# Block 0's rows and V's first weights loaded in two halves on two queues, and V's first steps split at 128 columns

## The chip, the cores and the metric

The kernel runs on one core of a Trainium2 chip. The metric is the device time of one execution in microseconds; the figure quoted for a kernel is the median of several runs.

## What is computed

A token block of 2048 rows and 512 columns in bf16 is layer-normalised and then goes through two mixers whose results are added to the input: a sliding dilated attention (32 heads of 16, a window of 8 positions 2 apart) and a gated MLP with a mixing over positions.

```python
xn = _layernorm(x)
# A: attention
q, k, v = split(xn @ wqkv)                     # 512 -> 3 x 512
logits = einsum('bhsd,bhswd->bhsw', q, kg) * Dh ** -0.5   # kg, vg: rows s, s-2, ..., s-14
o = einsum('bhsw,bhswd->bhsd', softmax(where(mask, logits, -1e9)), vg)
a = o @ wo
# B: gated MLP
z = gelu(xn @ w_in)                            # 512 -> 2 x 896
z1, z2 = z[..., :896], layernorm(z[..., 896:])
g = einsum('ts,bsf->btf', w_sp, z2) + b_sp     # 2048 x 2048 over positions
b = (z1 * g) @ w_out
out = x + a + b
```

## The kernel before

The 2048 rows are 16 blocks of 128 (`NB`), and four of them make a wave of 512 (`NJ` = 4). The program is a list of tasks. Each names its engine, what it reads and writes, an estimated duration and a priority. A planner (`Plan.schedule`, L123) places the tasks in an order for each engine, from the estimates and from given landing times of some loads (the dictionary at L1089), and `Plan.emit` writes that order out with semaphore waits. Extra order edges at L1073 to L1086 fix the sequence of the first steps by hand.

The work runs in these stages on TensorE: V's projection of the first blocks; the z2 half of the MLP's input (`z2_block`, L831); Q and K (`qk_pair`, L723); the z1 half (`z1_group`, L877); the rest of V (L700); the attention's reductions (L767); the mixing over positions (`g_group`, L977, the largest); and the output (`out_block`, L1033 and L1042). VectorE does the products of attention, ScalarE the evictions and activations, GpSimd some small steps and V's stores. Most loads go out on SyncE's queue (SP); ScalarE's queue carries two loads at the start and one store at the end.

What the change touches is the first five microseconds:

- Loads. ScalarE issues `ldx0` (L562, the 128 rows of block 0, 128 KB) and `ldx1` (L535). SP issues `ldwv0` and `ldwv1` (`ld_wv`, L539: V's weights, two halves of 256 KB; half `hf` holds the 128-row chunks 2 `hf` and 2 `hf` + 1), then `ldx2`, `ldx3`, `ldwin2a` and `ldwin2b` (L545, L551), `ldx4`, and then DMA transposes `xTd1` and on (L640). Each load has a semaphore of its own.
- Warm-up. TensorE runs seven matmuls on constants (L581; six of 512 columns, one of 128) and an eighth of 128 columns between the transposes and V's first step.
- ScalarE runs a priming activation (`actprime`, L585), before which its function table is loaded.
- Blocks 0 to 2 aren't normalised ahead of V: their raw rows are transposed on TensorE (`pe_tr`, L600) into PSUM, copied by ScalarE to the tile `xcT` (L628), and multiplied with V's weights (`v_block`, L700); mean and variance are put right later (`fix_all`, L751). The contraction over 512 columns goes in four chunks of 128, `dc` = 0 to 3.
- For block 0, `xTx0a` transposes chunks 0 and 1 and `xTx0b` chunks 2 and 3; `xTc0_0` and `xTc0_1` copy 256 columns each; `V0_0` multiplies chunks 0 and 1 (after `xTc0_0` and `ldwv0`), `V0_1` chunks 2 and 3 (after `xTc0_1` and `ldwv1`).
- TensorE's fixed order is: seven warm-up matmuls, `xTx0a`, `xTx0b`, the eighth, `V0_0`, `xTx1`, `V0_1`, `xTx2`, `V1_0`, `V1_1`, `xTr0`, `V2_0`, `V2_1`, then the z2 matmuls of the first blocks.
- VectorE takes statistics of each block (L620, L622), and GpSimd a power for the inverse deviation (L634).

Of the kernel before, what the change touches and what calls it, by code (L numbers as in the profile page):

```python
# [346 lines left out]
def build_kernel(nc, A_x, A_wqkv, A_wo, B_x, B_w_in, B_w_sp, B_b_sp, B_w_out, out, report=False, emit=True):  # L347
# [12 lines left out]
    NRAW = 3  # L360
    NWARM = 7
# [49 lines left out]
    with ExitStack() as es:  # L411
# [5 lines left out]
        def A(name, n, o2_=0):  # L417
            return ar[:, off[name] + o2_: off[name] + o2_ + n]
# [18 lines left out]
        def R1(key, name, n, o_=0):  # L437
            R(key, "sb", [(off[name] + o_, off[name] + o_ + n)])
# [117 lines left out]
        def ld_wqk(which, eng):  # L556
# [5 lines left out]
        dma("act", lambda e: e.dma_start(A("xin", 512), x2[0:128, :]), 128 * 512 * 2, ("xin", 0),  # L562
            writes=[("xin0", 0), ("xin0", 1)], name="ldx0")
        ld_x(1, "act")
        ld_wv(0)
        ld_wv(1)
        ld_x(2, "sp")
        ld_x(3, "sp")
# [45 lines left out]
        def ln_block(b):  # L614
            sl = b % 8
            xin = A("xin", 512, 512 * b)
            xn = A("xn", 512, 512 * sl)
            xk = [("xin", b)] if b else [("xin0", 0), ("xin0", 1)]

            T("dve", lambda v: v.bn_stats(Fv("st6", 6, 6 * b), xin), reads=xk, writes=[("st6", b)],  # L620
              est=685, name="bnst%d" % b, prio=b * 0.1)
            T("dve", lambda v: v.bn_aggr(Fv("mv", 2, 2 * b), Fv("st6", 6, 6 * b)), reads=[("st6", b)],  # L622
              writes=[("mv", b)], est=178, name="bnag%d" % b, prio=-1 + b * 0.1)
            if b < NRAW:
                bcs = [pe_tr(xin, xk, "xTx0a", (0, 1)), pe_tr(xin, xk, "xTx0b", (2, 3))] if b == 0 else [pe_tr(xin, xk, "xTx%d" % b)] * 2
                for h0, hn in ((0, 1), (1, 1)) if b < 2 else ((0, 2),):
                    bc = bcs[h0]
                    T("act", (lambda h0, hn, bc: lambda a: a.activation(A("xcT", 256 * hn, 512 * b + 256 * h0),  # L628
                                                                        P(bc, 256 * hn, 256 * h0), ACTF.Copy))(h0, hn, bc),
                      reads=[bc], writes=[("xcT", b, hf) for hf in range(h0, h0 + hn)], est=c_act(256 * hn),  # L630
                      name="xTc%d_%d" % (b, h0), prio=-1)
# [58 lines left out]
        def v_block(b):  # L690
            bk = plan.bank("V%d" % b)
            sl = b % 8
            vk = ("Vn", sl)
            vn = A("Vn" if sl < 4 else "bbc", 512, 512 * (sl % 4))

            for hf in range(2):
                def mm(t, hf=hf):
                    last = None
                    for dc in (2 * hf, 2 * hf + 1):
                        last = t.matmul(P(bk, 512), A("xcT", 128, 512 * b + 128 * dc) if b < NRAW else xTv(b, dc),  # L700
                                        A("wv", 512, 512 * dc), start=(dc == 0), stop=(dc == 3))
# [13 lines left out]
            v_write(b, vn, vk)  # L715
# [355 lines left out]

        byname = {t.name: t for t in plan.tasks}
        for names in (["warm%d" % wi for wi in range(NWARM)] +  # L1073
                      ["xTx0a", "xTx0b", "warm%d" % NWARM, "V0_0", "xTx1", "V0_1", "xTx2", "V1_0", "V1_1", "xTr0", "V2_0", "V2_1",
                       "z2_0_0", "z2_0_0b", "z2_0_1", "z2_1_0", "z2_1_1", "z2_2_0", "z2_2_1", "V3_0", "V3_1", "z2_3_0", "z2_3_1", "V4_0", "V4_1", "z2_4_0", "z2_4_1", "Q0_0", "Q0_1", "K0_0", "K0_1"],
                      ("rstd7", "Vw3"),
                      ("bnst0", "bnag0", "vpe0", "bnst1", "bnag1", "vpe1", "norm0", "bnst2", "norm1", "bnag2", "vpe2", "bnst3", "norm2",
                       "bnag3", "vpe3", "norm3", "bnst4", "bnag4", "vpe4", "mr", "norm4", "bnst5"),
                      ["bnst%d" % b for b in range(5, NB)],
                      ("xTc0_0", "xTc0_1", "xTc1_0", "xTc1_1", "xTc2_0", "xTe0_0", "xTe0_2", "Ve1", "Ve0", "Ve2",  # L1080
                       "z2g0", "z2g1", "z2s0"), ("ldx4", "xTd1", "xTd2", "xTd3", "xTd4", "ldq", "ldk", "ldx5", "ldx6", "ldx7", "ldwin1", "ldx8"), ("ldx15", "xTd5"),
                      *[("ldwin1", "ldx%d" % b) for b in range(9, NB)], *[("z2_4_1", "%s0_%d" % (n, c)) for n in "QK" for c in range(4)],
                      ("V10_1", "Q3_3"), ("csa", "csb", "csc", "csr", "ldwout"), ("csr", "ldwo0"), ("csr", "ldxr0"), ("csv", "zr3")):
# [4 lines left out]
        plan.schedule(tol=4.0, dma_bw=285.0, dma_lat=1600.0, overlap=60.0,  # L1088
                      land=dict(ldx0=3600.0, ldwv0=4120.0, ldx1=4550.0, ldwv1=5230.0, ldx2=5600.0, ldwin2a=7650.0, ldx3=6050.0,  # L1089
                                ldwin2b=8950.0, csa=75800.0, csb=78400.0, csc=83400.0, csr=86500.0, ldx4=9100.0, ldx5=18150.0, ldq=16300.0, xTd3=12130.0, ldk=17800.0, ldx6=18500.0, ldx7=18900.0, xTd4=13900.0, xTd1=9600.0, xTd2=10850.0, ldwin1=21500.0))  # L1090
        if report:
            print("arena", AR, "fp", FR)
# [12 lines left out]
        plan.landed = {("dve", "fin11_0"): [("wv", 0), ("wv", 1), "w_in2a", "w_in2b", "w_in1", "bbc", "w_out", "wo", ("xin", 0), ("xin", 1), ("xin", 2), ("xin", 3), ("xin", 4), ("xin", 5), ("xin", 6), ("xin", 7), ("xin", 8), ("xin", 9), ("xin", 10), ("xin", 11), ("xin", 12), ("xin", 13), ("xin", 14), ("xin", 15), ("wv", 0), ("wv", 1), "w_in2a", "w_in2b", "w_in1", "bbc", "w_out", "wo", ("xin", 0)]}  # L1105
# [36 lines left out]
```

## Time and profile before

| | |
|---|---|
| median of 3 runs | 236.19 us (235.75, 236.23, 236.19) |
| the profiled execution | 236.54 us |
| its span | 235.3 us, 3002 instructions |
| TensorE matmuls | 232.4 us busy, 99% |
| VectorE | 207.3 us, 88% |
| ScalarE | 95.9 us, 41% |
| GpSimd | 29.4 us, 12% |
| transfers | 44.55 MB, mean 189 GB/s |

The span runs from the first to the last instruction of the core; the execution's time has some 1.2 us around it. A line of the profile names the engine (PE is TensorE, PEld its weight loads, DVE VectorE, ACT ScalarE, POOL GpSimd, SP SyncE; a small q marks an engine's sequencer or its DMA issue), the source line, the operation, what is written and read, the shape and the count. In a timeline the first number is the start and the second the stretch from the first start to the last end of the merged instructions. Matmuls are pipelined: one starts before the one before it has ended, so the step from start to start is shorter than the duration printed. In a list of waits the numbers are the total, the count and the longest, in us.

Landing times in the profile, from issue to landing: 2.8 us for `ldx0` (issued at 0.81 us); 3.3 and 3.9 for `ldwv0` and `ldwv1`; 3.8 as the median of `ldx2`, `ldx3` and `ldx4`; 4.5 and 5.2 for the two halves of the z2 weights. What the transfers moved was 27 GB/s in the second microsecond of the span, 217 in the third, 379 in the fourth and 372 in the fifth.

### The profile page before, as it was taken

The page shows a single profiled execution, that of the slowest core. Times are in us where ns is not written, and L with a number is a line of the kernel's source. Part 1 is how long each engine was busy: PE and PEld are TensorE (multiplying, and loading weights), DVE is VectorE, ACT ScalarE, POOL GpSimd, SP SyncE. Part 2 cuts the span into 40 slices and gives each one's busy share as a digit, 9 for nine tenths or more (in the row PEclk, how much of TensorE's full clock was granted, in tenths as well). Part 3 has the DMA queues.
Part 4 walks back from the last instruction along what each step waited for, and adds up shares of the span by engine and source line. Part 5 has one row for each costly group of instructions (what it writes and reads, how often), then busy time and mean ns, then how long its engine had stood idle before and what let it go on. Part 6 is the DMA issues. An engine that isn't in the chain of part 4 may idle for free.

```text
span 235.3 us, 3002 instructions
## 1 busy us (share of the span) xinstructions
PE 232.4 (99%) x1127; PEld 109.0 (46%) x1127; DVE 207.3 (88%) x271; ACT 95.9 (41%) x143; POOL 29.4 (12%) x58
## 2 busy tenths in 40 slices
PE   8999999999999999999999999999999999999996
PEld 3545445544454444444444444444444444444443
DVE  4706899999999999999899999998899998999723
ACT  3788878888986679610120531111111111000000
POOL 2305740404361202000000000000000000000000
PEclk9999999999999999999999999999999999999999
DMA  6669934999911285346199999999969849945442
GB/s 221 203 193 368 181 68 103 215 202 214 228 45 50 67 231 173 66 94 175 58 353 239 273 212 266 195 236 288 279 180 306 269 145 303 288 115 156 111 137 68
DMA packets 83991, 44.55 MB, mean 189 GB/s; under 512 B 56180, under 2 KB 83204, under 8 KB 83976
## 3 DMA queue, kind: packets, MB, share of 16 engines
q1 hardware_dynamic: 82744, 41.94, 69.6%
q0 software_dynamic: 800, 2.11, 3.0%
q10 hardware_dynamic: 432, 0.30, 0.4%
q8 instruction: 9, 0.15, 0.3%
q14 instruction: 6, 0.05, 0.1%
HBM read 26.62 MB, written 4.22 MB: 131 GB/s over the span
## 4 chain that ended last, share of the span: by engine, by line
PE 98%; DVE 0%; ACT 0%; issue 0%; DVEq 0%
PE ps L977 41%; PE ps L723 12%; PE ps L831 10%; PE ps L877 10%; PE ps L1042 10%; PE ps L700 6%; PE ps L1033 6%; PE ps L581 1%; PE ps L767 1%; PE ps L600 1%; DVE arena L1048 0%; ACT arena L628 0%; PE ps L778 0%; DVEq L325 0%
## 5 line engine op out<-in xcount | busy, mean ns | idle before, releaser
L977 PE MATMUL ps<-arena 128*128 128x512 bf16 x448 | 97.0, 379 | 0.0
L977 PEld LDWEIGHTS ps<-arena 128*128 128x128 bf16 x448 | 43.8, 98 | 53.0 <-issue 0.4
L985 ACT ACTIVATE arena<-ps 128x1024 bf16<-128x1024 f32 (+1 forms) x16 | 14.7, 917 | 77.0 <-PE ps L977 70.6
L1005 DVE TENSOR_TENSOR arena<-arena 128x4096 bf16<-128x4096 bf16 x16 | 36.4, 2282 | 0.0
L744 DVE TENSOR_TENSOR arena<-arena 128x4096 bf16<-128x4096 bf16 x16 | 36.4, 2280 | 0.0
L1008 DVE TENSOR_TENSOR arena<-arena 128x2048 bf16<-128x2048 bf16 (+1 forms) x32 | 30.0, 948 | 0.2
L723 PE MATMUL ps<-arena 128*128 128x512 bf16 x128 | 28.8, 379 | 0.0
L749 DVE TENSOR_TENSOR arena<-arena 128x4096 bf16<-128x4096 bf16 x12 | 27.4, 2287 | 0.1
L1042 PE MATMUL ps<-arena 128*128 128x512 bf16 (+2 forms) x119 | 27.0, 366 | 0.0
L831 PE MATMUL ps<-arena 128*128 128x448 bf16 x128 | 25.5, 352 | 0.0
L877 PE MATMUL ps<-arena 128*128 128x512 bf16 x112 | 24.5, 379 | 0.0
L723 PEld LDWEIGHTS ps<-arena 128*128 128x128 bf16 x128 | 14.4, 113 | 13.3 <-ACT arena L713 0.4
L732 ACT ACTIVATE arena<-ps 128x1024 bf16<-128x1024 f32 x16 | 16.2, 1022 | 6.8 <-PE ps L723 6.6
L1048 DVE TENSOR_TENSOR arena<-ps,arena 128x512 bf16<-128x512 f32 (+2 forms) x17 | 11.2, 656 | 8.6 <-PE ps L1042 8.5
L831 PEld LDWEIGHTS ps<-arena 128*128 128x128 bf16 x128 | 12.5, 98 | 12.1 <-issue 0.2
L1042 PEld LDWEIGHTS ps<-arena 128*128 128x128 bf16 x119 | 11.4, 98 | 12.9
L877 PEld LDWEIGHTS ps<-arena 128*128 128x128 bf16 x112 | 11.0, 98 | 13.2
L700 PE MATMUL ps<-arena 128*128 128x512 bf16 x64 | 16.8, 395 | 0.2 <-ACT arena L628 0.2
L1033 PE MATMUL ps<-arena 128*128 128x512 bf16 (+2 forms) x68 | 16.6, 366 | 0.0
L839 ACT ACTIVATE arena<-ps 128x896 bf16<-128x896 f32 x16 | 14.6, 913 | 3.4 <-PE ps L831 3.3
L883 ACT ACTIVATE arena<-ps 128x1024 bf16<-128x1024 f32 (+1 forms) x16 | 14.0, 919 | 4.4 <-PE ps L877 4.3
L620 DVE BATCH_NORM_STATS2 fpool<-arena 128x6 f32<-128x512 bf16 x16 | 10.7, 685 | 5.5 <-DMA arena<-in_A_x_dram 5.5
(64 smaller groups left out, 168.2 us busy)
## 6 DMA issues: line engine op xcount, KB each, us to landing
arena<-vscr SPq DMA_DIRECT2D x16, 1024.0 KB, 6.1
arena<-in_A_x_dram SPq DMA_DIRECT2D x30, 128.0 KB, 3.8
vscr<-arena POOLq DMA_DIRECT2D x16, 128.0 KB, 3.9
out_dram<-arena SPq DMA_DIRECT2D x15, 128.0 KB, 2.0
arena<-in_A_wqkv_dram SPq DMA_DIRECT2D x2, 512.0 KB, 4.6
arena<-in_B_w_in_dram SPq DMA_DIRECT2D x2, 448.0 KB, 4.9
arena<-in_B_w_in_dram SPq DMA_DIRECT2D x1, 896.0 KB, 8.2
arena<-in_B_w_out_dram SPq DMA_DIRECT2D x1, 896.0 KB, 5.9
```

Source lines behind the costliest of these rows:

```text
L700: last = t.matmul(P(bk, 512), A("xcT", 128, 512 * b + 128 * dc) if b < NRAW else xTv(b, dc), A("wv", 512, 512 * dc), start=(dc == 0), stop ...
L723: last = t.matmul(P(bk, 512, 512 * which), AC(off["wqk"] + 2048 * which + 512 * dc + c, [[4, 128]]), AC(off["xnT"] + dc * S + 512 * j, [[1 ...
L732: T("act", lambda a: a.activation(AC(qo, [[ko - qo, 2], [1, 512]]), P(bk, 1024).rearrange("p (t n) -> p t n", t=2), ACTF.Copy, scale=0.5), ...
L744: T("dve", (lambda pbv, qb, kb: lambda v: v.tensor_tensor(pbv, qb, kb, ALU.mult))(pbv, qb, kb), reads=rd, writes=[("pb", s_)], est=c_tt(40 ...
L749: T("dve", (lambda av, bv: lambda v: v.tensor_tensor(av, av, bv, ALU.add))(av, bv), reads=[("pb", 1)], writes=[("pb", acc)], est=c_tt(4096 ...
L831: last = t.matmul(P(bk, 448, 512 * hf), xTv(b, dc), AC(off["w_in2"] + 896 * dc + 448 * hf, [[1, 448]]), start=(dc == 0), stop=(dc == 3))
L877: last = t.matmul(P(bk, 512, 512 * i), AC(off["w_in1"] + 896 * dc + 128 * fc, [[1, 128]]), AC(off["xnT"] + dc * S + 512 * j, [[1, 512]]), ...
L977: last = t.matmul(P(bk, 512, 512 * i), AC(off["z2"] + FH * sh + 128 * fc, [[1, 128]]), AC(off["wT%d" % r_] + sh * 512, [[1, 512]]), start= ...
L1005: T("dve", lambda v: v.tensor_tensor(tv, tv, av, ALU.mult), reads=[("attn", b)], writes=[("Vs", sv)], est=c_tt(4096), name="pv%d" % b, pri ...
L1008: T("dve", (lambda n: lambda v: v.tensor_tensor(A("Vs", n, 4096 * sv), A("Vs", n, 4096 * sv), A("Vs", n, 4096 * sv + n), ALU.add))(n), wri ...
L1033: last = t.matmul(P(bk, cn), AC(off["OT"] + 512 * tb + 128 * cc, [[1, 128]]), AC(off["wo"] + 512 * cc + c0, [[1, cn]]), start=(cc == 0), s ...
L1042: last = t.matmul(P(bk, cn), AC(off["z1T"] + fc * S + 128 * tb, [[1, 128]]), AC(off["w_out"] + 512 * fc + c0, [[1, cn]]), start=False, sto ...
```

## The change

Block 0's rows are loaded by two DMAs of 64 rows, the first issued by ScalarE (`ldx0a`), the second by SP (`ldx0b`). V's weights of chunk 0 follow on ScalarE's queue (`ldwvq0`, 128 KB) and those of chunk 1 on SP's (`ldwvq1`, 128 KB), in place of `ldwv0`. `ldx1` is then third on ScalarE's queue; `ldwv1` is third on SP's and what follows there moves one place back.

Block 0's first transposes are split: `xTx0a` does chunk 0, `xTx0b` chunk 1, `xTx0c` chunks 2 and 3, each into a PSUM bank of its own. ScalarE copies 128 columns twice (`xTc0_0a`, `xTc0_0b`) in place of 256 once; `xTc0_1` stays. `V0_0` becomes two tasks of one matmul, `V0_0` (chunk 0) and `V0_0b` (chunk 1), each waiting for its own copy and its own weights. The planner's landing times and the fixed order are adapted.

```diff
             R1(("wv", s_), "wv", 1024, 1024 * s_)
+            R1(("wvq", s_), "wv", 512, 512 * s_)
...
+            R1(("xcTq", hf), "xcT", 128, 128 * hf)
...
-        dma("act", lambda e: e.dma_start(A("xin", 512), x2[0:128, :]), 128 * 512 * 2, ("xin", 0),
-            writes=[("xin0", 0), ("xin0", 1)], name="ldx0")
+        for hf, eng in enumerate(("act", "sp")):
+            dma(eng, (lambda hf: lambda e: e.dma_start(A("xin", 512)[64 * hf:64 * hf + 64, :],
+                                                       x2[64 * hf:64 * hf + 64, :]))(hf), 64 * 512 * 2, ("xin0", hf),
+                writes=[("xin0", hf)], name="ldx0%s" % "ab"[hf])
+        for c, eng in enumerate(("act", "sp")):
+            dma(eng, (lambda c: lambda e: e.dma_start(A("wv", 512, 512 * c), A_wqkv[128 * c:128 * c + 128, 1024:1536]))(c),
+                128 * 512 * 2, ("wvq", c), writes=[("wvq", c)], name="ldwvq%d" % c)
         ld_x(1, "act")
-        ld_wv(0)
         ld_wv(1)
...
-                bcs = [pe_tr(xin, xk, "xTx0a", (0, 1)), pe_tr(xin, xk, "xTx0b", (2, 3))] if b == 0 else [pe_tr(xin, xk, "xTx%d" % b)] * 2
-                for h0, hn in ((0, 1), (1, 1)) if b < 2 else ((0, 2),):
-                    bc = bcs[h0]
+                bcs = [pe_tr(xin, xk, "xTx0a", (0,)), pe_tr(xin, xk, "xTx0b", (1,)), pe_tr(xin, xk, "xTx0c", (2, 3))] if b == 0 else [pe_tr(xin, xk, "xTx%d" % b)] * 2
+                for c0 in (0, 1) if b == 0 else ():
+                    T("act", (lambda c0, bc: lambda a: a.activation(A("xcT", 128, 128 * c0), P(bc, 128, 128 * c0), ACTF.Copy))(c0, bcs[c0]),
+                      reads=[bcs[c0]], writes=[("xcTq", c0)], est=c_act(128), name="xTc0_0%s" % "ab"[c0], prio=-1)
+                for h0, hn in ((1, 1),) if b == 0 else ((0, 1), (1, 1)) if b < 2 else ((0, 2),):
+                    bc = bcs[-1 if b == 0 else h0]
...
-            for hf in range(2):
-                def mm(t, hf=hf):
+            for hf, dcs, sfx in ((0, (0,), ""), (0, (1,), "b"), (1, (2, 3), "")) if b == 0 else ((0, (0, 1), ""), (1, (2, 3), "")):
+                def mm(t, dcs=dcs):
...
-                T("pe", mm, reads=[("xcT", b, hf) if b < NRAW else ("xnT", b), ("wv", hf)], writes=[bk],
-                  est=2 * c_mm(512) , name="V%d_%d" % (b, hf), prio=(2 if b < 4 else 60 + b))
+                T("pe", mm, reads=([("xcTq", dcs[0]), ("wvq", dcs[0])] if b == 0 and hf == 0 else
+                                   [("xcT", b, hf) if b < NRAW else ("xnT", b), ("wv", hf)]), writes=[bk],
+                  est=len(dcs) * c_mm(512), name="V%d_%d%s" % (b, hf, sfx), prio=(2 if b < 4 else 60 + b))
...
-                      ["xTx0a", "xTx0b", "warm%d" % NWARM, "V0_0", "xTx1", "V0_1", "xTx2", ...
+                      ["xTx0a", "xTx0b", "xTx0c", "warm%d" % NWARM, "V0_0", "V0_0b", "xTx1", "V0_1", "xTx2", ...
...
-                      land=dict(ldx0=3600.0, ldwv0=4120.0, ldx1=4550.0, ldwv1=5230.0, ...
+                      land=dict(ldx0a=3400.0, ldx0b=3400.0, ldwvq0=4100.0, ldwvq1=4100.0, ldx1=4550.0, ldwv1=5230.0, ...
```

More of the change, by code (lines that the diff above doesn't have):

```diff
@@ L694, in v_block @@
             vn = A("Vn" if sl < 4 else "bbc", 512, 512 * (sl % 4))
-            for hf in range(2):
-                def mm(t, hf=hf):
+            for hf, dcs, sfx in ((0, (0,), ""), (0, (1,), "b"), (1, (2, 3), "")) if b == 0 else ((0, (0, 1), ""), (1, (2, 3), "")):
+                def mm(t, dcs=dcs):
                     last = None
-                    for dc in (2 * hf, 2 * hf + 1):
+                    for dc in dcs:
                         last = t.matmul(P(bk, 512), A("xcT", 128, 512 * b + 128 * dc) if b < NRAW else xTv(b, dc),
@@ L1073, in build_kernel @@
         for names in (["warm%d" % wi for wi in range(NWARM)] +
-                      ["xTx0a", "xTx0b", "warm%d" % NWARM, "V0_0", "xTx1", "V0_1", "xTx2", "V1_0", "V1_1", "xTr0", "V2_0", "V2_1",
+                      ["xTx0a", "xTx0b", "xTx0c", "warm%d" % NWARM, "V0_0", "V0_0b", "xTx1", "V0_1", "xTx2", "V1_0", "V1_1", "xTr0", "V2_0", "V2_1",
                        "z2_0_0", "z2_0_0b", "z2_0_1", "z2_1_0", "z2_1_1", "z2_2_0", "z2_2_1", "V3_0", "V3_1", "z2_3_0", "z2_3_1", "V4_0", "V4_1", "z2_4_0", "z2_4_1", "Q0_0", "Q0_1", "K0_0", "K0_1"],
@@ L1088, in build_kernel @@
         plan.schedule(tol=4.0, dma_bw=285.0, dma_lat=1600.0, overlap=60.0,
-                      land=dict(ldx0=3600.0, ldwv0=4120.0, ldx1=4550.0, ldwv1=5230.0, ldx2=5600.0, ldwin2a=7650.0, ldx3=6050.0,
+                      land=dict(ldx0a=3400.0, ldx0b=3400.0, ldwvq0=4100.0, ldwvq1=4100.0, ldx1=4550.0, ldwv1=5230.0, ldx2=5600.0, ldwin2a=7650.0, ldx3=6050.0,
                                 ldwin2b=8950.0, csa=75800.0, csb=78400.0, csc=83400.0, csr=86500.0, ldx4=9100.0, ldx5=18150.0, ldq=16300.0, xTd3=12130.0, ldk=17800.0, ldx6=18500.0, ldx7=18900.0, xTd4=13900.0, xTd1=9600.0, xTd2=10850.0, ldwin1=21500.0))
@@ L1104, in build_kernel @@
         plan.final_hooks = {"sp": sp_final}
-        plan.landed = {("dve", "fin11_0"): [("wv", 0), ("wv", 1), "w_in2a", "w_in2b", "w_in1", "bbc", "w_out", "wo", ("xin", 0), ("xin", 1), ("xin", 2), ("xin", 3), ("xin", 4), ("xin", 5), ("xin", 6), ("xin", 7), ("xin", 8), ("xin", 9), ("xin", 10), ("xin", 11), ("xin", 12), ("xin", 13), ("xin", 14), ("xin", 15), ("wv", 0), ("wv", 1), "w_in2a", "w_in2b", "w_in1", "bbc", "w_out", "wo", ("xin", 0)]}
+        plan.landed = {("dve", "fin11_0"): [("wvq", 0), ("wv", 1), "w_in2a", "w_in2b", "w_in1", "bbc", "w_out", "wo", ("xin", 1), ("xin", 2), ("xin", 3), ("xin", 4), ("xin", 5), ("xin", 6), ("xin", 7), ("xin", 8), ("xin", 9), ("xin", 10), ("xin", 11), ("xin", 12), ("xin", 13), ("xin", 14), ("xin", 15), ("wvq", 0), ("wv", 1), "w_in2a", "w_in2b", "w_in1", "bbc", "w_out", "wo", ("xin", 1), ("xin", 2)]}
         with nc.allow_low_precision("bf16 intermediates by design"):
```

2 lines of the change are left out of this document (1 added, 1 removed).

## The prediction

> **What bounds the kernel now.** I read the busy shares first, then the chain that ended last, then the waits, then the first ten microseconds in order of time.
>
> ```profile
> PE 232.4 (99%) x1127; PEld 109.0 (46%) x1127; DVE 207.3 (88%) x271; ACT 95.9 (41%) x143; POOL 29.4 (12%) x58
> ...
> PE 98%; DVE 0%; ACT 0%; issue 0%; DVEq 0%
> ```
>
> TensorE is busy for 232.4 of 235.3 us and is 98% of the chain. Its idle 2.9 us must lie somewhere; the waits name where it begins:
>
> ```profile
> PE ps L581 <- PEq L1127: 0.8, 1, 0.8
> ...
> PE ps L700 <- ACT arena L628: 0.2, 1, 0.2
> ```
>
> 0.84 us pass before the first warm-up matmul, 0.16 us before V's first matmul, and no other wait of its matmuls is listed (weight loads lie under matmuls); the remaining 1.9 us are the tail behind its last matmul (230.0 to 235.3: 3.39 busy of 5.30). So a gain can only come from starting real work sooner, or from TensorE working faster.
>
> The front, in order of time (start, duration, engine, line):
>
> ```profile
> 0.80 0.97 SPq L539 DMA_DIRECT2D arena<-in_A_wqkv_dram  x2
> ...
> 0.81 0.41 ACTq L562 DMA_DIRECT2D arena<-in_A_x_dram  x1
> 0.84 2.83 PE L581 MATMUL ps<-const-bfloat16-1.0 128*128 128x512 bf16 x7 [0.84 <-PEq L1127]
> ...
> 1.74 1.28 ACT L585 ACT_TABLE_LOAD   x1 [1.74 <-PEq L1127]
> ...
> 3.03 0.20 ACT L585 ACTIVATE fpool<-fpool 128x4 f32<-128x4 f32 x1
> ...
> 3.62 0.61 PE L600 MATMUL ps<-arena 128*128 128x128 bf16 x4
> ...
> 4.05 0.66 ACT L628 ACTIVATE arena<-ps 128x256 bf16<-128x256 f32 x2 [0.81 <-PE ps L600]
> ...
> 4.49 1.04 PE L700 MATMUL ps<-arena 128*128 128x512 bf16 x2 [0.16 <-ACT arena L628]
> ```
>
> Block 0's rows land at 3.60 (issued 0.81, 2.8 to landing); four transposes from 3.62; ScalarE copies the first two out of PSUM from 4.05; V0 starts at 4.49. Until 3.62 TensorE does warm-up, which is no work; from there it is never without something to do for long.
>
> The last view is TensorE's V matmuls by form, first from 4.4 to 6.5 us, then from 7 to 8.8 us:
>
> ```profile
> L700 PE MATMUL ps<-arena 128*128 128x512 bf16 x4 | 2.1, 628 | 0.2 <-ACT arena L628 0.2
> ```
>
> ```profile
> L700 PE MATMUL ps<-arena 128*128 128x512 bf16 x8 | 2.1, 379 | 0.0
> ```
>
> The same matmul takes 628 ns early and 379 ns later, and one starts every 0.42 us (5.75, 6.17, 6.60) against every 0.216 us (four in 0.86). The granted clock is printed as 1.00 throughout, so the durations must be read. Block 2's four transposes take 0.33 us from 6.60 to 6.93, where four slow ones would take 0.43 and four fast ones 0.22: two of each, so the switch lies near **6.82 us**. This halves what an early gain is worth: a microsecond of slow work done before the switch stands for half a microsecond afterwards.
>
> **The change, step by step.**
>
> *Rows of block 0 in two halves.* Before, the 128 KB shared the engines with 256 KB of V's weights issued 0.01 us earlier on the other queue; now both queues carry rows first, then weights. Bytes bound the landing: 27 KB had moved by 2.0 us, 217 more by 3.0, then 379 per us. If rows and weights shared equally, the rows were through with 256 KB moved (3.03 us); alone in front they need 128 KB (2.47). So the landing lies between 3.60 (nothing won, the same engines) and 3.60 - 0.56 = 3.04. I take 3.4, nearer the upper end, since SP's half has to start up on a queue of its own. The value hardly matters: the last short warm-up matmul ends its row at 3.66 (2.92 + 0.74) with a duration of 0.31, so it starts at 3.35 and frees the array 0.107 later. Transposes start at **3.46** for any landing before that; gain 0.16.
>
> The Trainium skill speaks against this step: "DMA: Bandwidth & Descriptors", section "Rules for kernel authors", says that two transfers to disjoint partition halves aren't worth making, because both spread over the same 16 engines. By that rule the rows land at 3.60 as before, and the sum below would be 0.09 in place of 0.17 us. No row of this trace splits a load, so it stays open until the run.
>
> *One transpose, one copy of 128 columns.* The copy started 0.43 us behind the first of two transposes; with one it is 0.107 less. A copy of 256 columns takes 0.381, one of 512 takes 0.597, so 128 columns come to 0.381 - 0.108 = 0.27. Both are on the path: 0.10 + 0.11. The second copy and the third (block 0's upper half) follow while V0's first matmul runs 0.42 us. The extra copy costs ScalarE about 0.2 us in a place where it had been idle 1.28 us next.
>
> So V0 can start at 4.49 - 0.16 - 0.10 - 0.11 = 4.12, if its weights are there. Before they landed at 4.1 (0.80 + 3.3). The first quarter is now second on ScalarE's queue, issued near 1.25, with the same 384 KB in all up to the end of both quarters: 4.1 by bytes. The other bound is the 128 KB that were second on that queue before (x1, issued 1.25, 3.3 to landing): 4.55. I take 4.15, by bytes, because the transfers run at 379 GB/s from 3 to 4 us and 372 from 4 to 5, so it is bytes and not issues that they wait for. **V0 at 4.15, 0.34 us sooner**, with 4.57 (0.08 later) as the bad end.
>
> *Moved behind it.* x1 is issued third on ScalarE (about 1.70 for 1.25); on SP every load from wv1 to x4 moves one issue back, 0.45 to 0.5 us. In steps of slow work: V0's second matmul 4.57, x1's transposes 5.00, V0's upper half 5.42, x2's transposes 6.27, V1 6.70. x1 landed at 4.55 and may take the 0.45 whole: 5.00, just in time. wv1 landed at 1.31 + 3.9 = 5.2, x2 at 1.82 + 3.8 = 5.6; bytes in front of both are unchanged, and with 0.45 more they would be 5.65 and 6.05, which costs at most 0.23 of slow time at V0's upper half. w_in2b lands at 3.27 + 5.2 = 8.47 (8.92 at worst) and is wanted at about 9.6; the first DMA transposes issued at 6.96 land 2.5 later, 9.5, wanted near 10.4. None of these binds.
>
> *ScalarE's third issue* pushes the table load from 1.74 to about 2.2 and the priming activation to 3.49 to 3.69; the first copy is wanted at 3.8. That cover is 0.1 us; a later table load would hand its excess to V0 at half price. VectorE's statistics wait for both halves and only move up.
>
> *Behind the front* the instruction order of all five engines is the same in both programs but for the split steps; PSUM bank numbers differ.
>
> **Sum.** 0.34 us of slow work gained up to the switch is 0.34 x 0.216/0.427 = 0.17 us afterwards, and since TensorE waits for nothing until its last matmul, it reaches the end: span 235.3 - 0.17 = 235.13. The profiled execution took 236.54, with 1.24 around its span, and is 0.35 above the median of the runs shown; applied to the median, 236.19 - 0.17 = **236.02**.
>
> **The rivals.**
>
> 1. *The halves land no sooner* (the change doesn't do what it says). For it: the same engines, the bytes unchanged. Against: 256 KB no longer share with the rows. V0 then starts at 4.49 - 0.21 = 4.28; 0.09 us gained: **236.10**.
>
> 2. *The switch lies elsewhere in the timed runs.* For it: 235.75 to 236.23 and 236.54 for one program; the trace shows no wait behind the front with room for 0.8 us, while each microsecond by which the switch comes sooner saves 0.49. The fastest run, 0.44 under the median, would have it 0.9 us sooner. If most runs after fall there, the median is 235.75 less 0.09 to 0.17: **235.62**. Against: two of three runs shown lie at 236.2.
> The Trainium skill, "TensorE: Matmul & The Clock Gate", section "What's actually happening", says that a monitor frees the clock after a busy window of about 3.4 us that runs free of the kernel's start. The early and late durations here agree; whether the place varies from run to run, one trace can't show.
>
> 3. *Slower: x1 lands late.* Place: x1's transposes, which ran at 5.32; price: half of every microsecond past that, and it decides from a landing after 5.32. If x1, now third on its queue and level with wv1 and x2, lands only with x2 at 5.6 plus that load's own 0.45 delay, 6.05, it costs 0.73 of slow time, 0.36: **236.55**. Against: its bytes stand in front of x2's.
>
> 4. *Slower: the break before V0 grows and the switch waits for another stretch of work.* It came 5.98 us after the first matmul, with breaks of 0.16 at most. Counted anew from V0 at 4.15 it comes at 10.1: 3.3 us more at half rate, 1.62 lost against the 0.17 gained, **237.6**. Against: transposes and the filler matmul reach to 4.0, so the break is about as long as before.
>
> **How the numbers follow.** Forecast 0.45, rival 1 0.17, rival 2 0.18, rival 3 0.10, rival 4 0.06, an unforeseen stall 0.04. A measurement of this kernel can't tell less than about 0.2% (0.47 us) from no change: faster means under 235.72, slower over 236.66. Faster: 0.16 of rival 2. Slower: rivals 4 and the unforeseen whole, 0.02 of rival 3. Same: the rest, 0.72. The range 235.55 to 236.50 holds the forecast, rival 1, nearly all of rival 2 and the milder half of rival 3, and leaves out under 0.2.
>
> **What would show it.** Right: block 0's transposes from about 3.46, ScalarE's first copy 0.27 us long, V0's first matmul near 4.15, no new wait of TensorE before 6.8, x1's transposes near 5.0. Wrong: a wait of V0 for its weights rather than ScalarE; the table load ending past 3.6; matmuls still at 628 ns past 7 us; any wait of TensorE behind 10 us.

## The result, and the profile after

The changed kernel takes **238.40 us** as the median of five runs (237.94 to 238.67), beside 236.19 us for the kernel before on the same chip (235.75 to 236.24). The ratio is 1.0098 with a 95% interval of 1.0083 to 1.0113: about 2.2 us slower. The forecast of 236.02 and its range were wrong; slower had a chance of 0.12.

The busy shares and the chain that ended last, on the page of the changed kernel (238.51 us, span 237.2):

```profile
PE 232.6 (98%) x1107; PEld 109.7 (46%) x1127; DVE 207.7 (88%) x271; ACT 95.9 (40%) x144; POOL 29.4 (12%) x58
...
PE 96%; DMA 1%; issue 1%; DVE 0%; ACTq 0%; DVEq 0%
```

TensorE is as busy as before (232.4 us), but a DMA has come onto the chain. Where it stands shows in the front, in order of time (start, duration, engine, line; in brackets the idle time before and what ended it):

```profile
0.80 0.59 SPq L565 DMA_DIRECT2D arena<-in_A_x_dram  x1
...
0.81 0.57 ACTq L565 DMA_DIRECT2D arena<-in_A_x_dram  x1
...
1.42 0.59 ACTq L569 DMA_DIRECT2D arena<-in_A_wqkv_dram  x1
1.45 0.74 SPq L569 DMA_DIRECT2D arena<-in_A_wqkv_dram  x1
...
2.04 0.45 ACTq L537 DMA_DIRECT2D arena<-in_A_x_dram  x1
...
2.24 0.42 SPq L541 DMA_DIRECT2D arena<-in_A_wqkv_dram  x1
...
3.46 0.63 PE L606 MATMUL ps<-arena 128*128 128x128 bf16 x4
...
4.17 0.52 SPq L553 DMA_DIRECT2D arena<-in_B_w_in_dram  x1
...
4.91 1.04 PE L709 MATMUL ps<-arena 128*128 128x512 bf16 x2 [0.71 <-DMA arena<-in_A_wqkv_dram]
...
5.50 0.69 DVE L626 BATCH_NORM_STATS2 fpool<-arena 128x6 f32<-128x512 bf16 x1 [1.15 <-DMA arena<-in_A_x_dram]
```

The transposes begin at 3.46, where they were forecast. V's first matmul then waits 0.71 us for its weights and starts at 4.91, later than before (4.49). x1, issued at 2.04 instead of 1.25, is there at 5.50 instead of 4.55. The second half of the z2 weights (`ldwin2b`) is issued at 4.17 instead of 3.27, and lands 6.6 us later, at 10.8 instead of 8.47. V's matmuls by form, from 4.8 to 9.6 us (busy, mean ns), are still slow:

```profile
L709 PE MATMUL ps<-arena 128*128 128x512 bf16 x8 | 4.0, 623 | 0.7 <-DMA arena<-in_A_wqkv_dram 0.7
```

The switch to fast matmuls lies near 10.3 us in this execution; it was near 6.82 in the one shown of before. Q's first matmuls start at 20.12 us after and at 18.18 before, so 1.94 us are lost ahead of them; the spans differ by 1.9. All of the loss is in the front. Two causes offered themselves there, the later loads and the later switch, and the experiments are to part them.

### The profile page after: what moved, and what is told of

Its sections match the earlier page's. It is cut to its first block, busy times and chain, and to the rows that moved or that the text cites. A ratio compares the mean times of both kernels' runs of the same rounds, so it can differ in the third digit from the quotient of the medians.

```text
span 237.2 us, 2986 instructions
## 1 busy us (share of the span) xinstructions
PE 232.6 (98%) x1107; PEld 109.7 (46%) x1127; DVE 207.7 (88%) x271; ACT 95.9 (40%) x144; POOL 29.4 (12%) x58
## 3 DMA queue, kind: packets, MB, share of 16 engines
q0 software_dynamic: 800, 2.11, 3.0%
## 4 chain that ended last, share of the span: by engine, by line
PE 96%; DMA 1%; issue 1%; DVE 0%; ACTq 0%; DVEq 0%
PE ps L987 41%; PE ps L733 12%; PE ps L841 10%; PE ps L887 10%; PE ps L1052 10%; PE ps L709 7%; PE ps L1043 6%; DMA arena<-in_A_wqkv_dram 1%; PE ps L777 1%; PE ps L606 1%; DVE arena L1058 0%; ACTq L565 0%; PE ps L788 0%; DVEq L325 0%
## 5 line engine op out<-in xcount | busy, mean ns | idle before, releaser
L1052 PE MATMUL ps<-arena 128*128 128x512 bf16 (+2 forms) x116 | 26.5, 366 | 0.1
L1043 PE MATMUL ps<-arena 128*128 128x512 bf16 (+2 forms) x68 | 16.6, 366 | 0.1
L626 DVE BATCH_NORM_STATS2 fpool<-arena 128x6 f32<-128x512 bf16 x16 | 10.8, 688 | 6.0 <-DMA arena<-in_A_x_dram 5.9
```

The costliest lines, as they stand in the source:

```text
L1043: last = t.matmul(P(bk, cn), AC(off["OT"] + 512 * tb + 128 * cc, [[1, 128]]), AC(off["wo"] + 512 * cc + c0, [[1, cn]]), start=(cc == 0), s ...
L1052: last = t.matmul(P(bk, cn), AC(off["z1T"] + fc * S + 128 * tb, [[1, 128]]), AC(off["w_out"] + 512 * fc + c0, [[1, cn]]), start=False, sto ...
```

## The experiments

A useful measure came out of the first profiles: the start of block 1's z2 matmuls (`z2_1_0`), the ninth matmul of the z2 line. In the chains below it is the start of the group "x16". In the two profiles first shown TensorE comes to it without a break, eight steps of 0.19 us behind block 0's first (8.88 and 10.83). What follows it took about the same time:

| run | block 1's z2 starts | time of that run | difference |
|---|---|---|---|
| before, once more | 9.68 | 235.83 | 226.15 |
| before, as first shown | 10.40 | 236.54 | 226.14 |
| columns_and_quarters | 10.63 | 236.79 | 226.16 |
| weights_quarters_only | 10.86 | 237.08 | 226.22 |
| after_filled | 11.51 | 237.68 | 226.17 |
| late_issue_only | 11.57 | 237.75 | 226.18 |
| after, once more | 11.77 | 237.94 | 226.17 |
| after, as first shown | 12.34 | 238.51 | 226.17 |

So a kernel's time can be explained by what delays that one step. Of the twelve other profiles ten give 226.11 to 226.21; row_halves_on_scalar (226.40) and filled_z2_sooner (227.29) have one more wait of TensorE behind it.

### Each part alone

**steps128_only**: loads as before, only the split steps.

```diff
+                bcs = [pe_tr(xin, xk, "xTx0a", (0,)), pe_tr(xin, xk, "xTx0b", (1,)), pe_tr(xin, xk, "xTx0c", (2, 3))] if b == 0 else [pe_tr(xin, xk, "xTx%d" % b)] * 2
...
+            for hf, dcs, sfx in ((0, (0,), ""), (0, (1,), "b"), (1, (2, 3), "")) if b == 0 else ((0, (0, 1), ""), (1, (2, 3), "")):
```

> The loads of the kernel before (block 0's rows whole on ScalarE, V's first weights whole first on SP) with the changed steps: one transpose, one copy of 128 columns, one matmul at a time. Theory L (all of the loss comes from the loads): V's first matmul starts about 0.2 us sooner relative to the landing of the rows, 4.2 to 4.3, and the time is 235.9 to 236.1. Rival (the split steps cost time themselves, by further waits and a third bank): 236.5 or more.

Median 236.14 (235.74 to 236.52), ratio 0.9997 [0.9984, 1.0010]. Within 0.3 us either way the split steps cost nothing and bring nothing. The load experiments made from the changed kernel keep them, so that their differences are those of the loads.

**x0_halves_only**: the rows in two halves; V's first weights whole, second on SP.

```diff
+        for hf, eng in enumerate(("act", "sp")):
+            dma(eng, (lambda hf: lambda e: e.dma_start(A("xin", 512)[64 * hf:64 * hf + 64, :],
+                                                       x2[64 * hf:64 * hf + 64, :]))(hf), 64 * 512 * 2, ("xin0", hf),
         ld_x(1, "act")
         ld_wv(0)
```

> The changed kernel, but V's first weights come whole again: one load of 256 KB second on SP, none on ScalarE between the row half and block 1's rows; the steps of 128 columns stay. Theory A (the two row halves cost the time: each takes 0.57 to 0.59 us to issue where the whole took 0.41, and the first packets move 0.3 us later): the weights land past 4.7 us, V starts at 4.8 or later and the time stays near 238.4. Theory B (the two weight loads from two queues cost it): the rows land near 3.3, V starts at 4.2 to 4.5, the matmuls turn fast at 6.8 us, and the time is 236.0 to 236.2.

Median 237.81 (236.82 to 238.28), ratio 1.0067 [1.0047, 1.0088]. The rows land at 3.24, but V's first weights, issued at 1.45, only 3.9 us later; V0 starts at 5.36 after a wait of 1.16. `ldwin2b`, issued at 4.28 behind them, lands at 10.53; block 0's last four z2 matmuls wait for it to 10.58, and block 1's, at 11.51, for their transpose. Matmuls were already fast when V0 began, so the loads alone did this.

**weights_quarters_only**: the rows whole on ScalarE; V's first weights in two quarters, second on ScalarE and first on SP.

```diff
+        for c, eng in enumerate(("act", "sp")):
+            dma(eng, (lambda c: lambda e: e.dma_start(A("wv", 512, 512 * c), A_wqkv[128 * c:128 * c + 128, 1024:1536]))(c),
         ld_x(1, "act")
-        ld_wv(0)
```

> The changed kernel, but block 0's rows come in one load on ScalarE again; V's first weights stay in two loads, second on ScalarE and first on SP. Theory A (the row halves cost the time): V starts at 4.5 or sooner, the time is 236.0 to 236.2. Theory B (the two weight loads cost it): the transfers between 3.0 and 4.5 us stay under 300 GB/s, V waits for its weights past 4.7 and the time stays near 238.4.

Median 237.48 (237.07 to 239.02), ratio 1.0072 [1.0049, 1.0096]. Neither part alone is harmless. Here the chain runs through x1, third on ScalarE's queue (start, duration, what):

```profile
1.72 4.32 DMA arena<-in_A_x_dram
...
8.43 2.38 DMA arena<-arena
...
10.86 3.20 PE ps L839 x16
```

x1 lands at 6.04. VectorE takes its statistics and normalises blocks 0 and 1, a DMA transpose of block 1 is issued at 8.43, and the x16 is block 1's z2, which waits for it.

### The switch

**after_filled**: the changed kernel with seven more matmuls on constants before V0, so that TensorE has no break there.

```diff
-        for wi in range(NWARM + 1):
+        for wi in range(NWARM + 1 + 7):
```

> The changed kernel with seven more matmuls on constants, 128 columns each, in front of V's first step, where TensorE stood idle 0.71 us; loads as in the changed kernel. Theory C (the break before V makes the matmuls turn fast one stretch of 3.4 us later): V still starts near 4.9, but the matmuls turn fast near 6.8 us instead of 10.3; then the late second half of the z2 weights (10.8 us, wanted at 9.6 before) is the next wait, and the time is 236.8 to 237.5. Rival D (the switch comes late for another reason, or the lateness of the loads alone sets the time): the switch stays near 10.3 and the time at 238.4.

**before_gap**: the kernel before, with V0 also waiting for the second half of V's weights; its loads are untouched.

```diff
+        byname["V0_0"].deps.add(byname["ldwv1"])
```

> The kernel before with one wait more: V's first step also waits for the second half of V's weights (5.2 us), so TensorE stands idle about 0.85 us in front of it; every load and every order as before. Theory C: the matmuls turn fast near 10.2 us; V starts 0.7 us later and 3.4 us more run at half rate: span up by 2.0 us, time 238.0 to 238.4. Rival D: the switch stays at 6.8 us, the later start costs 0.71 at half rate, 0.36: time 236.5.

after_filled: three runs of five at 237.56 to 237.68, the others at 238.49 and 239.36; ratio 1.0085 [1.0056, 1.0115]. The break is gone and the switch is near 5.9, 4.4 us sooner than in the profile of after, but TensorE's timeline shows z2 waiting:

```profile
4.74 1.06 PE L709 MATMUL ps<-arena 128*128 128x512 bf16 x2
...
10.54 2.27 PE L841 MATMUL ps<-arena 128*128 128x448 bf16 x10 [0.27 <-DMA arena<-in_B_w_in_dram]
```

So with an early switch the loads still hold the time at about 237.6. before_gap: seven runs of ten at 236.08 to 236.55 like the kernel before, three at 237.78, 238.22 and 238.53; ratio 1.0029 [1.0002, 1.0055]. The profiled one is the slowest (TensorE's timeline):

```profile
5.16 1.03 PE L700 MATMUL ps<-arena 128*128 128x512 bf16 x2 [0.95 <-DMA arena<-in_A_wqkv_dram]
...
9.83 1.21 PE L700 MATMUL ps<-arena 128*128 128x512 bf16 x4
10.88 2.05 PE L831 MATMUL ps<-arena 128*128 128x448 bf16 x10
```

Loads came as before and no z2 matmul waited, yet matmuls were slow to about 10.2. A break can thus put the switch back and cost some 1.6 to 2.4 us by itself (beside 236.16, the median of the other seven), but only in some executions. Of the three long ones this alone is profiled; none of 20 runs of the kernel before, beside it, was over 236.54.

**before_again** and **after_again**: both kernels unchanged, one execution each, to see whether the place of the switch repeats.

> The kernel before once more, for a second profile. If the place of the switch moves freely: not at 6.8 us as in the first profile (236.54) but sooner, and a time under 236.54 that is lower the sooner it lies, by 0.5 us for each microsecond as long as no load is waited for. If the place is fixed: 6.8 us and 236.5 again. Full rate of the transfers from 3 us in either case.

> The changed kernel once more, for a second profile of it. If the slow transfers belong to the kernel: again under 300 GB/s from 3 to 4.5 us, V's weights past 4.7 us. If the place where the matmuls turn fast moves freely from execution to execution but a break in front of V puts it back by a stretch: a place other than 10.3 us is possible, and the time follows it, down to 237.6 (the run with fillers) where it is before 6.5 us.

235.83 and 237.94 us. It doesn't repeat: this time both switched early, near 3.6 and 3.9 us. That makes the pair the cleanest comparison of the case. First the chain of before, then that of after:

```profile
8.13 1.54 PE ps L831 x8
...
9.68 3.20 PE ps L831 x16
```

```profile
2.03 3.59 DMA arena<-in_A_x_dram
...
5.65 0.70 DVE fpool L626
...
8.01 3.71 DMA arena<-arena
...
11.77 3.20 PE ps L841 x16
```

At the same switch, times differ by 2.11 and the starts of block 1's z2 by 2.09. Before, block 1's z2 follows block 0's without a break. After, it waits for a transpose that began late (8.01 for 6.88, since x1 came at 5.62 for 4.52) and took 3.71 us to land, where the first of before_again took 2.8. The z2 weights came late as well (`ldwin2b` issued at 4.26 for 3.27), and block 0's last four z2 matmuls waited for them (TensorE's timeline of after_again):

```profile
10.79 0.93 PE L841 MATMUL ps<-arena 128*128 128x448 bf16 x4 [0.17 <-DMA arena<-in_B_w_in_dram]
```

Behind these four, at steps of 0.19 us, block 1's z2 could not have started before about 11.55 (an estimate) even with its transpose there. So the late weights alone would cost most of the 2.09 us, and an earlier x1 alone would win back about 0.2.

### What makes a load late

**row_halves_on_scalar**: both halves of the rows on ScalarE, SP's queue as before.

```diff
+        for hf in range(2):
+            dma("act", (lambda hf: lambda e: e.dma_start(A("xin", 512)[64 * hf:64 * hf + 64, :],
```

> Both halves of 64 rows issued by ScalarE, one behind the other; SP's queue as in the kernel before (first and second half of V's weights, then blocks 2 and 3, then the z2 weights); steps of 128 columns. Theory S (each load put in front of others on SP moves all that follow there, and the z2 weights end up as the wait): SP issues the second half of the z2 weights near 3.3 again, it lands by 8.6, no wait at the z2 matmuls, 236.0 to 236.4. Theory R (loads of 64 rows slow the transfers behind them, whatever the queue): transfers under 300 GB/s between 3 and 4.5 us, time 237 or more.

**quarters_on_sync**: V's first weights in two quarters, both on SP, the rows as before.

```diff
+        for c, eng in enumerate(("sp", "sp")):
-        ld_wv(0)
```

> Rows of block 0 whole, and ScalarE's queue as in the kernel before; V's first weights in two loads of 128 KB, both first on SP; steps of 128 columns. Theory S: one load more on SP, so the second half of the z2 weights is issued 0.45 to 0.5 us later and lands near 8.9 to 9.1, still in time: 236.0 to 236.5. Theory R: no load of 64 rows, so full rate from 3 us as before: 236.0. Theory X (what hurt the kernel with whole rows and quarters was block 1's rows as ScalarE's third load, landing past 5.5): also 236.0 to 236.2, with block 1's rows at 4.6.

**column_halves**: the rows in two halves of 256 columns (128 rows each) in place of 64 rows, V's first weights whole, second on SP.

```diff
+            dma(eng, (lambda hf: lambda e: e.dma_start(A("xin", 256, 256 * hf),
+                                                       x2[0:128, 256 * hf:256 * hf + 256]))(hf), 64 * 512 * 2, ("xin0", hf),
```

> Block 0's rows in two halves from the two queues as in the run with row halves only, but halves of 256 columns by 128 rows instead of 64 rows by 512 columns; V's first weights whole, second on SP. Theory R (the form of 64 rows is the trouble): issues of 0.41 to 0.45 again, full rate from 3 us, 236.0 to 236.5. Theory S (a further load in front on SP, whatever its form): the second half of the z2 weights issued 0.45 or more later, V's weights past 4.5 us, 236.8 to 237.8, as with row halves.

**columns_and_quarters**: the whole change, with halves of 256 columns in place of 64 rows.

> The changed kernel, but the halves of block 0's rows are 256 columns by 128 rows; quarters of V's weights as in the changed kernel. Theory R (the 64-row form carries most): issues of 0.41 to 0.45 in place of 0.57 to 0.59, the second half of the z2 weights issued 0.4 us sooner than in the changed kernel and landed by 9.5, floor of the runs (fast early) 236.8 or less. Theory S (one load more on each queue in front, whatever its form): V's weights past 4.7 us, most runs 237.6 or more.

row_halves_on_scalar: 237.84 (237.32 to 239.02), ratio 1.0075 [1.0055, 1.0096]. With SP untouched the loss is still there: the second half is issued at 1.40 and lands at 5.32, block 0's transposes wait 1.71 us. Neither theory's reason held: `ldwin2b` was issued at 3.26 and no z2 matmul of block 0 waited for it, but the fourth microsecond moved 358 GB/s.

quarters_on_sync: 236.97 (236.33 to 238.47), 1.0038 [1.0016, 1.0059]; one place more on SP, and `ldwv1`, issued at 1.71 for 1.31, lands at 6.32 for 5.2 in the profiled run, the slowest; the median is above what any of the three theories gave.

column_halves: four runs of ten at 236.27 to 236.59, the others at 237.79 to 238.66; 1.0055 [1.0027, 1.0082]. columns_and_quarters: 237.11 (236.79 to 238.41), 1.0060 [1.0032, 1.0088].

Issuing a load of 64 rows took 0.55 to 0.59 us, one of 128 rows of half the width 0.39 to 0.41. The loads of 128 rows issued right behind 64 rows were slow as well: 0.59 to 0.83 us, where the same loads took 0.39 to 0.48 elsewhere. In the whole change the column form cost less (1.0060 beside 1.0098, some 0.9 us, though the intervals just overlap), but is still slower than before: x1 is third on ScalarE's queue in either form, and lands at 5.78.

**block1_second**: as columns_and_quarters, with x1 second and V's first quarter third on ScalarE's queue.

```diff
         ld_x(1, "act")
+        for c, eng in ((0, "act"),):
+            dma(eng, (lambda c: lambda e: e.dma_start(A("wv", 512, 512 * c), A_wqkv[128 * c:128 * c + 128, 1024:1536]))(c),
```

> The run with column halves and quarters, with block 1's rows second and the quarter of V's weights third on ScalarE. If the chain from block 1's rows (landing, statistics, normalisation, DMA transpose, z2 of block 1) set the end there (start of block 1's z2 at 10.6 us, time 236.8): block 1's rows land near 4.6, that start falls to 10.0 or less, fastest runs 236.1 to 236.4, though V now starts past 5. If not: 236.8 or more.

Three runs of ten at 236.63 to 236.85, seven at 237.94 to 238.88; ratio 1.0074 [1.0049, 1.0098]. Now x1 lands at 4.2, and the quarter is what comes late. Its chain:

```profile
1.72 4.12 DMA arena<-in_A_wqkv_dram
...
5.88 0.61 PE ps L712 x2
```

The load that stands third on that queue, issued near 1.72, takes 4.05 to 4.32 us from issue to landing in these kernels (x1 in two above, the quarter here). Second there, issued at 1.25, x1 of before took 3.3. The next section shows that the third place alone isn't the reason. Changing the order moved the lateness, here to V0 itself after a wait of 1.69.

**filled_z2_sooner**: after_filled with block 3's rows behind the z2 weights on SP, an attempt to win the loss back.

```diff
-        ld_x(3, "sp")
...
+        ld_x(3, "sp")
```

> The run with fillers (seven more matmuls on constants in front of V, loads as in the changed kernel), with block 3's rows issued behind the z2 weights instead of in front. Theory L (what is left of the loss with the switch early is the wait of the z2 matmuls for the second half of their weights, landed at 10.5): it is issued 0.47 us sooner and has 128 KB less in front, lands near 9.7, and the time falls to 236.9 to 237.2. Rival (the time hangs on something else behind the front): 237.6 as with fillers alone.

It was slower, not faster: 238.10 (238.01 to 238.36), ratio 1.0092 [1.0076, 1.0108]. Block 1's z2 did start sooner, at 11.07 for 11.51, but x3 now lands at 10.06 and its transpose, issued at 11.12, at 13.41, with a z2 block behind it at 13.55. The wait moved to the load that was put back.

### The slot or the bytes

**tiny_on_sync**, **tiny_on_scalar**, **tiny_on_both**: the kernel before with loads of 512 bytes, of numbers that nothing uses, put in where the change puts its own: two on SP (before and after `ldwv0`), one on ScalarE (between x0 and x1), or all three. **tiny16_on_sync**: two on SP as well, of 64 bytes from 16 rows.

```diff
+        tiny(0, "sp")
         ld_wv(0)
+        tiny(1, "sp")
```

> The kernel before with two loads of 512 bytes on SP, one in front of the first half of V's weights and one behind it; they fetch numbers that nothing uses. SP's later loads are issued about 0.9 us later, as in the changed kernel; the bytes are those of before. Slots alone explain the lateness: the second half of the z2 weights, issued near 4.2, lands past 10 us, V's weights past 4.5, time 237 or more. The transfers explain it: the queues stay full, the second half lands by 8.9, V's weights near 4.4, time 236.1 to 236.5.

> The kernel before with one load of 512 bytes on ScalarE between block 0's and block 1's rows, which makes block 1's rows the third load there, issued near 1.7. Slots alone: block 1's rows land past 5.2, its DMA transpose past 10.2, time 236.6 or more. Transfers: they land by 4.8, 236.0 to 236.3.

> Both: two loads of 512 bytes on SP and one on ScalarE, the issue pattern of the changed kernel without its split loads. Slots alone: near the changed kernel, 237.6 to 238.4, fastest runs not under 237.3. Transfers: 236.1 to 236.6; the remaining 1.5 us and more then belong to the split loads themselves.

> As the run with two tiny loads on SP, but each of 16 packets (64 bytes) in place of 128 packets (512 bytes). If the packets of the tiny loads cost: 236.0 to 236.5. If the slot of a load on its queue costs, whatever it carries: 237 or more, as with 128 packets.

| run | median (range) | ratio [95%] | what is late |
|---|---|---|---|
| tiny_on_sync | 237.75 (236.67 to 238.51) | 1.0056 [1.0035, 1.0077] | V0 waits 0.68; `ldwin2b` issued 4.16 |
| tiny16_on_sync | 237.89 (237.65 to 238.09) | 1.0077 [1.0062, 1.0092] | V0 waits 0.68; `ldwin2b` issued 4.17 |
| tiny_on_scalar | 236.58 (236.37 to 238.26) | 1.0033 [1.0012, 1.0054] | x1 issued 1.74, lands 6.00 |
| tiny_on_both | 237.41 (236.91 to 238.44) | 1.0060 [1.0032, 1.0087] | `ldwv1` lands 6.72, V0's upper half waits 1.66 |

On SP, loads of almost no bytes cost more than half of what the change costs; a part of that comes through late switches (in both profiles with loads on SP alone matmuls are slow to about 9.7, behind the wait of 0.68). Issuing one took about as long as issuing a real load (0.39 to 0.46 us), and 16 rows were no better than 128.

In tiny_on_both x1 is third on ScalarE's queue too, and issued as early as in tiny_on_scalar, but it is there at 4.72 and not at 6.00:

```profile
1.73 0.47 ACTq L538 DMA_DIRECT2D arena<-in_A_x_dram  x1
...
4.72 0.69 DVE L630 BATCH_NORM_STATS2 fpool<-arena 128x6 f32<-128x512 bf16 x1 [0.66 <-DMA arena<-in_A_x_dram]
```

What differs is SP's queue: it had handed out `ldwv0` alone ahead of x1, where in tiny_on_scalar it had handed out `ldwv1` too. Over all the profiles, x1 took 2.4 to 3.64 us from issue to landing, second or third, where both queues had handed out at most 384 KB ahead of it, and 4.05 to 4.32 where they had handed out 640 KB or more. No run varied this alone.

**late_issue_only**: the kernel before with no load added or split; SP issues `ldwv1` only after the third warm-up matmul, and all behind it on SP's queue comes later with it.

```diff
+        byname["ldwv1"].deps.add(byname["warm2"])
+        byname["ldwv1"].start = byname["warm2"].start + 1
```

> The kernel before, in which the issue of the second half of V's weights on SP waits for the third warm-up matmul; SP's later loads then go out about 1 us later (the second half of the z2 weights near 4.2 in place of 3.27), with no further load and the same bytes. If the late issue is what costs: V's upper half waits, the second half of the z2 weights lands near 10, time 236.9 to 237.8, as with the two tiny loads on SP. If a further load costs by itself: it lands by 9.2, time 236.0 to 236.6.

237.71 (237.58 to 238.47), ratio 1.0078 [1.0056, 1.0099]. `ldwv1` goes out at 2.31 for 1.31, and its chain is nearly that of after_again:

```profile
2.75 4.02 DMA arena<-in_A_x_dram
...
6.79 0.70 DVE fpool L620
...
7.83 3.70 DMA arena<-arena
...
11.57 3.20 PE ps L831 x16
```

It is x2 here, since VectorE's fixed order has x2's statistics ahead of block 1's normalisation. With the same transfers and the same sizes, issuing one queue's loads a microsecond later costs 1.7 us. What the transfers moved by microsecond (stretch, its length, granted clock, share of the 16 engines' time, GB/s), for before_again and then for late_issue_only:

```profile
3.00:4.00 1.00, 1.00 1.09 381
4.00:5.00 1.00, 1.00 1.06 371
```

```profile
3.00:4.00 1.00, 1.00 0.89 303
4.00:5.00 1.00, 1.00 0.64 153
```

The hole follows the hole in the issues. Up to 1.31 us late_issue_only had handed out x0, `ldwv0` and x1, 524 kB, and by 4.0 us 536 kB had moved (26 + 207 + 303). The changed kernel had handed out 393 kB by 1.45, and 385 kB had moved by 4.0 (0 + 209 + 176). The kernel before had handed out 786 kB by 1.31; 623 kB had moved (27 + 217 + 379), and its transfers were the only ones of the three that ran full.

## Why the prediction was wrong

*Rows, transposes, copies*: right. The rows landed at 3.25 (forecast 3.4, before 3.60), the transposes began at 3.46 as forecast, and ScalarE's two copies of 128 columns took 0.42 together, the second 0.27. The Trainium skill ("DMA: Bandwidth & Descriptors", "Rules for kernel authors") holds two halves for not worth making. The rows did land 0.35 us sooner (0.25 in the second pair), but V's weights had moved behind them as well, so this is no test of the page's reason; for the kernel's time its advice stands (x0_halves_only, 1.0067). Rival 1, that the halves land no sooner, is out; its sum was also off, since 0.21 us at 0.216/0.427 are 0.11 and not 0.09.

*ScalarE's third issue*: the table load ended at 3.80 (forecast 3.49), and the cover of 0.1 us was used up. It cost nothing in the profile of after, as V0 waited for its weights to 4.91; in after_again, with the first quarter there in time, V0's first matmul waited 0.28 for ScalarE, about what that wait was in before_again (0.31).

*V0 at 4.15 "by bytes"*: **failed**. The count of bytes in front was right, the rate was not. I took the transfers for limited by bytes because they ran at 379 GB/s before. By the comparison above they ran so because 786 kB were handed out by 1.31 us. With half of that, the fourth microsecond moved 176, and V's first quarter landed at 4.87, past even the bad end of 4.57. In after_again it landed near 4.3, but chunk 1's quarter only near 5.1, and V's second matmul waited 0.42 us for it.

*"Moved behind it … None of these binds"*: **the step that decided**. Two things were mis-sized in it. The delay of the issues was put at 0.45 to 0.5 us; it was 0.79 for x1 (2.04 for 1.25) and 0.90 to 0.93 for `ldwv1`, `ldwin2a` and `ldwin2b`, since SP issues two loads in place of one ahead of `ldwv1`, and those were slow (0.59 and 0.74). And landings were taken to move by no more than the issue: `ldwin2b` was given 8.92 at worst and came at 10.8; the first DMA transpose was given 9.5 and came at 11.7 in after_again. late_issue_only shows that the late issue suffices for this: there `ldwin2b` and a late transpose held block 1's z2 to 11.57.

*Rival 3, x1 lands late*: the right load and condition (over 5.32; it landed at 5.50 and 5.62), but the wrong reader, and a price of 0.36 us against a loss of about 2.1, which the z2 weights shared. I followed x1 to its first reader, TensorE's transposes, and not through VectorE's fixed order of statistics and normalisations and the DMA transpose to block 1's z2.

*Rival 4, the switch waits for another stretch*: its mechanism is real. It forecast the switch at 10.1; the profile of after has it at 10.3, behind a break of 0.71, and before_gap shows such a switch with the loads untouched. That the number fits is luck: counted from V0, as the rival did, its 5.98 us would give 10.9 in that profile (V0 at 4.91) and 11.1 in before_gap, where the switch came at 10.2. Nor is it what the change costs at the least: after_again switched at 3.9 and still lost 2.11. The two don't add up, since both push the same step: the loads hold block 1's z2 to 11.77, the late switch to 12.34, and the later one counts, 0.57 in that start and 0.57 in the times.

*Rival 2, the switch lies elsewhere from run to run*: true of its premise. The switch lay at 3.6 us in one profile of before and at 6.8 in the other. The Trainium skill ("TensorE: Matmul & The Clock Gate", "What's actually happening") speaks of a window of about 3.4 us that runs free of the kernel's start. The places in all 20 profiles fit that, at 3.6 to 6.8 or 9.3 to 10.3 us, but don't show the length: the 3.46 us from 6.82 to 10.28 lie between two executions. But I priced a microsecond of earlier switch at 0.49, and it brought 0.22 (0.71 us of time for 3.2): with faster matmuls before_again waits for ScalarE and for `ldwv1` (0.31 and 0.25). The kernel before thus stood close to its loads already, which the profile with the late switch hid. That is why "wanted near 10.4" for the transposes was no safe margin; with the early switch block 1's z2 started at 9.68.

*Split steps*: they cost nothing that shows (0.9997), and their forecast gain of about 0.1 us is smaller than that interval can tell.

What stays open. Whether a given break puts the switch back varies from run to run (3 of 10 in before_gap), and no run fixes how long a break it takes; late places (9.3 or later) were seen only in profiles with a break of 0.56 us or more in or before V's first steps, and other profiles with such breaks switched early. How often the changed kernel's own runs switch late isn't known beyond its two profiles. Within a microsecond, the transfer rates weren't explained, and that a load lands late because of what was handed out ahead of it rests on comparing kernels. That the DMA transpose lands late (3.7 us) because other loads are still under way is an argument, not shown by a run of its own: in weights_quarters_only, columns_and_quarters and row_halves_on_scalar, where `ldwin2b` had landed by about 9.3, a transpose issued at 8.16 to 8.72 took 2.4. No version tried beat the kernel before; steps128_only equals it.

## What to carry to other kernels

Count the issues in front of every later load, each at its measured time, before splitting a load: here a place on a queue was worth more than the bytes, and the transfers ran below their rate when less was handed out early. Follow a late load to its last reader through every fixed order on the way, not only to its first. And take more than one profile of a kernel whose matmuls change speed on the way: a slow start can cover how close the loads are.

## What the runs showed of the hardware

- Issuing a load took about the same time for 64 bytes (0.40 and 0.46 us) as for 128 KB in 128 rows (0.39 to 0.51 us), and longer for 64 rows of 1 KB (0.55 to 0.59 us) and for the load right behind those (0.59 to 0.83 us).
- Block 1's rows, on ScalarE's queue, landed 2.4 to 3.64 us after their issue where at most 384 KB had been handed out ahead on both queues, and 4.05 to 4.32 us where it was 640 KB or more; third on the queue they took 3.0 us in one kernel (tiny_on_both) and 4.26 in another (tiny_on_scalar).
- A hole of 1 us in the issues of one queue (late_issue_only) left the transfers at 153 GB/s in one later microsecond, in place of 371, and cost 1.7 us of time.
- The place where matmuls double their speed lay at 3.6 to 6.8 us or at 9.3 to 10.3 us in the profiles of nearly the same front, with the granted clock printed as 1.00 throughout.
